# Holding input loads and a weight load behind two transposing transfers, and rearranging one quad on GpSimd

## The chip, the cores and the metric
The kernel runs on one core of a Trainium2 chip. The metric is the device time of one execution in microseconds (us). The core has TensorE (PE, matmuls; PEld is its weight load), VectorE (DVE), ScalarE (ACT), GpSimd (POOL) and SyncE (SP), and 16 DMA engines that all queues share. Three runs of the kernel before took 386.72, 385.92 and 386.15 us, so the median is 386.15 us.

## The reference
An attention with squared relu, then a two-layer block whose middle is a leaky relu with a slope for each channel:

```python
# q, k, v: 8 batches x 12 heads x 448 positions x 64
scores = scale * (q @ k^T)
attn = maximum(scores, 0) ** 2 / 448
x = (attn @ v), heads side by side           # 3584 tokens x 768
h = x @ w_in                                 # 768 -> 2048
g = maximum(h, 0) + alpha * minimum(h, 0)
out = g @ w_out                              # 2048 -> 768, float32
```

## The kernel before
The unit of attention is a **quad**: four heads of one batch, so three quads for each batch and 24 in all. `load_qk(n)` and `load_v(n)` (lines 94 and 103) bring a quad's q, k and v from HBM; GpSimd issues these DMAs, and they turn float32 into bf16 on the way. Each tensor of a quad is 224 KB in bf16. The buffers `raw` for q and k are three deep each, `v` seven deep.

The scores need q and k with the 64 channels on the partitions. The first five quads are transposed on TensorE (`turn_pe`, line 149). From quad 5 on it is `turn_dma` (line 161): VectorE copies q and k into a buffer `perm` in another order of rows (line 164, two copies), then SyncE issues one transposing DMA from `perm` to a tile `T` (line 166). `perm` has two buffers, `T` four. The text calls the tile of quad 5 T[5], and so on.

`sc` computes score chunks: four matmuls (line 178) and a relu on ScalarE or VectorE (lines 187 and 189). `sq` squares them (line 197 on VectorE, line 195 on ScalarE). `attnv(n)` multiplies by v (line 207) and evicts half of the result on ScalarE (line 217) and half on VectorE (line 218) into `xT`. `f1(b, ff)` is the first layer for 128 of 2048 channels (matmuls at line 241, `f1_out` at lines 249 and 250). `f2(sb, c, h)` is the second layer for 128 tokens and one of two column groups of the output, h = 0 being the first 256 columns and h = 1 the other 512 (matmuls at line 266, 16 for each group, then a ScalarE copy at line 268 and two output DMAs from SyncE at line 274). The weights of h = 1 are the tile `w_out1`, loaded by `load_w_out(1)` (line 120) in four DMAs of 512 KB, of which each serves four of the 16 matmuls of a group in turn.

The order of the work is written out by hand; each engine takes its instructions in program order, and one that waits holds up all behind it. GpSimd's stream holds nearly only DMA issues. Line 376 is the exception: a copy of one element of T[5] into the tile `landed`. It has no other use than that GpSimd waits there until the transposing transfer of quad 5 is complete, and that what stands behind it on GpSimd is issued later. Before this copy stand the loads of q and k of quad 6 and q of quad 7 (lines 374 and 375); behind it k of quad 7, quad 8, `load_w_out(1)`, and v of quad 6.

Around the change, TensorE does this (lines 368 to 446): f1 of batch 0 to its end, f2(0,0,0), scores of quad 4, attnv(3), f2(0,1,0), f2(0,2,0), scores of quad 5 (the first use of T[5], line 396), attnv(4), the beginning of f1 of batch 1 (lines 418 to 421; it reads xT of quads 3 and 4), the rest of quad 5, attnv(5), f1 of batch 1, f2(0,3,0), scores of quad 6 (line 440, the first use of T[6]), f2(0,0,1) (line 441, the first use of w_out1). The transposing transfers of quads 7 and 8 are called from inside f1 of batch 1 (line 436).

The lines of the section that the change touches:

```python
    load_qk(6)
    load_qk(7, "q")
    nc.gpsimd.tensor_copy(landed, T[5][:1, 0, 0, :1])
    load_qk(7, "k")
    load_qk(8)
    load_w_out(1)
    load_v(6)
```

Of the kernel before, what the change touches and what calls it, by code (L numbers as in the profile page):

```python
# [20 lines left out]
def kernel(  # L21
# [10 lines left out]
    nc = tc.nc  # L32
# [12 lines left out]
    singles = ctx.enter_context(tc.tile_pool(name="singles", bufs=1))  # L45
    raw_pool = ctx.enter_context(tc.tile_pool(name="raw", bufs=3))
    v_pool = ctx.enter_context(tc.tile_pool(name="v", bufs=7))
    perm_pool = ctx.enter_context(tc.tile_pool(name="perm", bufs=2))
    T_pool = ctx.enter_context(tc.tile_pool(name="T", bufs=4))
    rl_pool = ctx.enter_context(tc.tile_pool(name="rl", bufs=7))  # L50
    at_pool = ctx.enter_context(tc.tile_pool(name="at", bufs=12))
# [11 lines left out]
    landed = singles.tile([1, 1], BF16)  # L63
# [22 lines left out]
    def take_bank():  # L86
        i = min(range(8), key=lambda i: (taken[i], i))
        take(i, 1)
        return psum[:, i]


    raw, vraw = {}, {}

    def load_qk(n, names="qk"):
        b, g = divmod(n, NG)
        for name in names:
            src = q if name == "q" else k
            t = raw_pool.tile([128, 2, NJ, D], BF16, tag=name, name=f"{name}raw")
            flat = src[b].rearrange("(m two) (pp j) d -> (two pp) m (j d)", two=2, j=NJ)
            nc.gpsimd.dma_start(out=t.rearrange("p m j d -> p m (j d)"), in_=flat[:, 2 * g:2 * g + 2])  # L100
            raw[(n, name)] = t

    def load_v(n):
        b, g = divmod(n, NG)
        t = v_pool.tile([128, 2, NJ, D], BF16, tag="v", name="vraw")
        flat = v[b].rearrange("(m two) (pp j) d -> (two pp) m (j d)", two=2, j=NJ)
        nc.gpsimd.dma_start(out=t.rearrange("p m j d -> p m (j d)"), in_=flat[:, 2 * g:2 * g + 2])  # L107
        vraw[n] = t
# [11 lines left out]
    def load_w_out(h, lo=0, hi=KF, step=4):  # L120
        for lo in range(lo, hi, step):
            nc.gpsimd.dma_start(out=w_out_sb[h][:, lo:lo + step], in_=w_out_v[:, lo:lo + step, COLS[h][0]:COLS[h][1]])
# [24 lines left out]
    T = {}  # L147
# [10 lines left out]
            copy = nc.vector.tensor_copy if eng == "D" else nc.scalar.copy  # L158
            copy(dst, ps[:, 128 * lo:128 * hi])  # L159

    def turn_dma(n):
        p = perm_pool.tile([128, 2, NJ, 2, D], BF16, tag="perm", name="perm")
        for i, name in enumerate("qk"):
            nc.vector.tensor_copy(p[:, i], raw.pop((n, name)).rearrange("p s j d -> p j s d"))  # L164
        t = T_pool.tile([128, 2, NJ, 128], BF16, tag="T", name="T")
        nc.sync.dma_start_transpose(out=t.rearrange("p a j c -> p (a j) c"),
                                    in_=p.rearrange("p a j s d -> p (a j s d)"))
        T[n] = t
# [53 lines left out]
    def sc(chunks):  # L222

        for n, j, eng in chunks:
            late.append((n, j, relu(score_mm(n, j), eng)))

    def sq(k=99, eng="D"):
        for g in late[:k]:
            square(*g, eng)
        del late[:k]  # L230
# [28 lines left out]
    def f2(sb, c, h, parts=None):  # L259

        first_col, width = COLS[h][0], COLS[h][1] - COLS[h][0]
        o = o_pool.tile([128, d_model - CUT], F32, tag="o", name="osb")
        for lo, hi in parts or ((0, width),):
            ps = take_bank()[:, :hi - lo]
            for ff in range(KF):
                nc.tensor.matmul(ps, gT[sb][:, ff, bass.ts(c, 128)], w_out_sb[h][:, ff, lo:hi],  # L266
                                 start=(ff == 0), stop=(ff == KF - 1))
            nc.scalar.copy(o[:, lo:hi], ps)  # L268
            for u in range(2):
                blk = 2 * c + u  # L270
                b, j = 2 * sb + blk // NJ, blk % NJ
                rows = out[b * S:(b + 1) * S].rearrange("(pp j) d -> j pp d", j=NJ)
                eng = nc.scalar if u and parts else nc.sync
                eng.dma_start(out=rows[j][:, first_col + lo:first_col + hi], in_=o[64 * u:64 * u + 64, lo:hi])  # L274
# [4 lines left out]
    def ch(n, lo, hi, p=pat):  # L279
        return [(n, j, p[j]) for j in range(lo, hi)]  # L280
# [61 lines left out]
    def f1s(b, lo, hi):  # L342
        for ff in range(lo, hi):
            f1(b, ff)
# [6 lines left out]
    def prepare(n):  # L351
        if n < NQ:
            turn_dma(n)
        load(n + 2)
# [11 lines left out]
    f1s(0, 10, 12)  # L366
    sc(ch(3, 6, 7) + ch(4, 0, 2, "AA"))
    turn_dma(5)
    f1s(0, 12, 13)
    kept = late[:]  # L370
    del late[:]
    f1s(0, 13, 16)
    late += kept
    load_qk(6)
    load_qk(7, "q")
    nc.gpsimd.tensor_copy(landed, T[5][:1, 0, 0, :1])
    load_qk(7, "k")
    load_qk(8)
    load_w_out(1)
    load_v(6)  # L380
    f2(0, 0, 0)
    sq()
    sc(ch(4, 2, 5, "AAADAAA"))
# [2 lines left out]
    sq(3)  # L386
    sq(2, "A")
    sq()
    turn_dma(6)
    load_qk(9)  # L390
    load_v(7)
    load_v(8)
    load_v(9)
    f2(0, 1, 0)
    f2(0, 2, 0)
    sc(ch(5, 0, 3))
    sq(1)
    attnv(4)
# [117 lines left out]
```

## Time and profile before
| | |
|---|---|
| median of three runs | 386.15 us (385.92 to 386.72) |
| the profiled execution | 386.72 us |
| its span | 384.8 us, so 1.92 us lie around it |
| DVE, ACT, POOL busy | 266.0, 206.8 and 67.9 us |
| granted TensorE clock | 0.999 |
| T[5]: issued by SyncE, landed | at 43.33 us, 10.6 us later |
| T[6]: issued by SyncE, landed | at 53.71 us, 6.4 us later |
| last quarter of w_out1: landed | 17.1 us after its issue at about 58.9 us |

Times in the trace are counted from the span's start. A line of a timeline gives start, duration, engine, source line and operation, what is written from what, the number of instructions merged into it, and in brackets the idle time before it with what ended it. The list of waits gives the total, the number and the longest. The DMA view for a stretch of time gives, for each queue, its packets, megabytes and the share of the 16 engines' time: q0 carries the DMAs that GpSimd issues ("software"), q1 those of SyncE and ScalarE ("hardware"). Megabytes are those of the bf16 written.

### The profile page before, as it was taken

The numbers are of one execution on the slowest core, as the hardware profiler recorded it, in microseconds if no ns is written. First come the engines' busy times: TensorE is split into PE (matmuls) and PEld (weight loads), VectorE is DVE, ScalarE is ACT, GpSimd is POOL, SyncE is SP. The second block draws the span as 40 slices with busy tenths as digits, with TensorE's granted clock in tenths as the row PEclk, the third lists the DMA queues.
The fourth block names the chain that finished last, engine by engine and source line by source line (L and its number), as shares of the span: only waits on it lengthen the run. The fifth ranks groups of instructions, "written<-read, shape, count | busy, mean of one in ns | idle before, by whom it ended". The sixth has DMA issues, their size and how long they took to land.

```text
span 384.8 us, 7838 instructions
## 1 busy us (share of the span) xinstructions
PE 374.6 (97%) x3178; PEld 205.4 (53%) x3200; DVE 266.0 (69%) x422; ACT 206.8 (54%) x331; POOL 67.9 (18%) x102
## 2 busy tenths in 40 slices
PE   7799999999999999999999999999999999999996
PEld 6444554545554455545465455544556445645554
DVE  4987987765777988689655897779855788526300
ACT  5978686446364664565444655537544375434321
POOL 8557235132202202022200222020000000000000
PEclk9999999999999999999999999999999999999999
DMA  9999999999993666698292872946035300120023
GB/s 160 189 202 201 201 129 207 176 193 227 179 191 49 113 123 102 110 141 119 45 162 61 140 122 46 171 67 127 17 82 91 77 0 16 43 68 2 14 68 84
DMA packets 73284, 43.42 MB, mean 113 GB/s; under 512 B 40352, under 2 KB 69792, under 8 KB 73248
## 3 DMA queue, kind: packets, MB, share of 16 engines
q0 software_dynamic: 26864, 22.45, 39.6%
q1 hardware_dynamic: 45952, 20.07, 27.0%
q8 instruction: 25, 0.41, 0.4%
q10 hardware_dynamic: 432, 0.39, 0.3%
q14 instruction: 11, 0.09, 0.1%
HBM read 45.62 MB, written 11.01 MB: 147 GB/s over the span
## 4 chain that ended last, share of the span: by engine, by line
PE 89%; DMA 6%; DVE 3%; issue 1%; ACT 0%; ACTq 0%
PE psum L266 37%; PE psum L241 36%; PE psum L178 8%; PE psum L207 8%; DMA T<-perm 3%; DMA kraw<-in_k_dram 2%; DVE at L197 2%; DMA qfirst<-in_q_dram 1%; PE psum L156 1%; DVE T L159 1%; DVE rl L189 1%; ACT osb L268 0%; ACTq L274 0%; DVE qraw L140 0%; ACT T L159 0%
## 5 line engine op out<-in xcount | busy, mean ns | idle before, releaser
L266 PE MATMUL psum<-w_out,gT 128*128 128x256 bf16 (+3 forms) x890 | 149.8, 322 | 1.2
L241 PE MATMUL psum<-xT,w_in_sb 128*128 128x448 bf16 x768 | 150.0, 353 | 0.0
L266 PEld LDWEIGHTS <-gT 128*128 128x128 bf16 x912 | 86.7, 98 | 64.2 <-issue 8.2
L241 PEld LDWEIGHTS <-w_in_sb 128*128 128x128 bf16 x768 | 73.5, 98 | 73.0 <-issue 5.7
L250 DVE SCALAR_TENSOR_TENSOR gT<-neg,beta_sb,psum 128x448 bf16<-128x448 f32 x128 | 83.5, 677 | 35.8 <-ACT neg L249 35.8
L249 ACT ACTIVATE neg<-psum 128x448 f32<-128x448 f32 x128 | 69.2, 546 | 61.5 <-PE psum L241 60.3
L187 ACT ACTIVATE rl<-psum 128x896 bf16<-128x896 f32 x113 | 97.9, 931 | 2.2 <-PE psum L178 2.2
L197 DVE TENSOR_TENSOR at<-rl 128x896 bf16<-128x896 bf16 x164 | 91.6, 617 | 0.0
L189 DVE TENSOR_SCALAR rl<-psum 128x896 bf16<-128x896 f32 x55 | 59.7, 1086 | 40.0 <-PE psum L178 39.9
L268 ACT COPY osb<-psum 128x256 f32<-128x256 f32 (+3 forms) x57 | 26.9, 473 | 104.5 <-PE psum L266 98.7
L178 PE MATMUL psum<-T 64*64 64x448 bf16 x672 | 44.7, 356 | 3.6 <-DVE T L159 1.1
L100 POOL DMA_DIRECT2D qraw<-in_q_dram x23 | 16.6, 721 | 157.1 <-DVE perm L164 148.4
L207 PE MATMUL psum<-at,vraw 64*64 64x448 bf16 x672 | 36.6, 350 | 0.3 <-DVE at L197 0.2
L178 PEld LDWEIGHTS <-T 64*64 64x64 bf16 x672 | 16.6, 106 | 22.2 <-issue 12.5
L207 PEld LDWEIGHTS <-vraw 64*64 64x64 bf16 x672 | 20.9, 106 | 12.6 <-issue 2.3
L218 DVE TENSOR_SCALAR xT<-psum 128x448 bf16<-128x448 f32 x23 | 14.3, 624 | 14.5 <-PE psum L207 10.9
L107 POOL DMA_DIRECT2D vraw<-in_v_dram x24 | 17.5, 729 | 7.1 <-DMA w_out<-in_moe_w_out_dram 4.1
L100 POOL DMA_DIRECT2D kraw<-in_k_dram x23 | 16.6, 722 | 6.2 <-DMA w_out<-in_moe_w_out_dram 3.2
L217 ACT ACTIVATE xT<-psum 128x448 bf16<-128x448 f32 x23 | 12.6, 549 | 2.7 <-PE psum L207 2.7
L164 DVE COPY perm<-qraw 128x896 bf16<-128x896 bf16 x19 | 11.6, 611 | 0.0
L164 DVE COPY perm<-kraw 128x896 bf16<-128x896 bf16 x19 | 11.5, 608 | 0.0
L117 POOL DMA_DIRECT2D w_in_sb<-in_moe_w_in_dram x16 | 10.1, 633 | 7.4 <-DMA w_in_sb<-in_moe_w_in_dram 2.8
(25 smaller groups left out, 40.4 us busy)
## 6 DMA issues: line engine op xcount, KB each, us to landing
out_dram<-osb SPq DMA_DIRECT2D x54, 128.0 KB, 2.4
vraw<-in_v_dram POOLq DMA_DIRECT2D x24, 224.0 KB, 8.2
qraw<-in_q_dram POOLq DMA_DIRECT2D x23, 224.0 KB, 5.4
kraw<-in_k_dram POOLq DMA_DIRECT2D x23, 224.0 KB, 6.8
out_dram<-osb SPq DMA_DIRECT2D x56, 64.0 KB, 2.2
w_in_sb<-in_moe_w_in_dram POOLq DMA_DIRECT2D x16, 192.0 KB, 8.9
w_out<-in_moe_w_out_dram POOLq DMA_DIRECT2D x4, 512.0 KB, 12.4
w_out<-in_moe_w_out_dram POOLq DMA_DIRECT2D x4, 256.0 KB, 8.9
```

The source lines that it names most:

```text
L100: nc.gpsimd.dma_start(out=t.rearrange("p m j d -> p m (j d)"), in_=flat[:, 2 * g:2 * g + 2])
L164: nc.vector.tensor_copy(p[:, i], raw.pop((n, name)).rearrange("p s j d -> p j s d"))
L178: nc.tensor.matmul(ps[64 * c:64 * c + 64, r, :S], t[64 * r:64 * r + 64, 1, j, 64 * c:64 * c + 64], t[64 * r:64 * r + 64, 0, :, 64 * c:64 * ...
L187: nc.scalar.activation(rl, ps[:, :, :S], ACTF.Relu)
L189: nc.vector.tensor_scalar(rl, ps[:, :, :S], 0.0, None, ALU.max)
L197: nc.vector.tensor_tensor(a, rl, rl, ALU.mult)
L207: nc.tensor.matmul(ps[64 * s:64 * s + 64, r, :S], vv[64 * r:64 * r + 64, s, j, :], a[64 * r:64 * r + 64, s], start=(j == 0), stop=(j == NJ ...
L241: nc.tensor.matmul(ps, w_in_sb[:, km // 2, km % 2, bass.ts(ff, 128)], xT[b][:, km // 2, km % 2, :], start=(km == 0), stop=(km == KM - 1))
L249: nc.scalar.activation(neg, ps, ACTF.Relu, scale=-1.0)
L250: nc.vector.scalar_tensor_tensor(gT[b // 2][:, ff, (b % 2) * S:(b % 2) * S + S], neg, beta_sb[:, ff:ff + 1], ps, ALU.mult, ALU.add)
L266: nc.tensor.matmul(ps, gT[sb][:, ff, bass.ts(c, 128)], w_out_sb[h][:, ff, lo:hi], start=(ff == 0), stop=(ff == KF - 1))
L268: nc.scalar.copy(o[:, lo:hi], ps)
```

## The change
One buffer more for `perm`. The copy that waits for T[5] moves ahead of all loads of quads 6 to 8. The two copies that rearrange quad 6 are made by GpSimd, right behind these loads, and v of quads 6 and 7 is loaded behind them. The transposing transfer of quad 6 is issued behind f2(0,1,0) and f2(0,2,0), which puts it behind four output DMAs on SyncE. A second copy of one element into `landed` makes GpSimd wait for T[6]; w_out1 is loaded behind it, then quad 9 and v of quads 8 and 9. The streams of TensorE and ScalarE keep their order.

```diff
-    perm_pool = ctx.enter_context(tc.tile_pool(name="perm", bufs=2))
+    perm_pool = ctx.enter_context(tc.tile_pool(name="perm", bufs=3))
...
-    def turn_dma(n):
+    def rearrange_rows(n, eng):
         p = perm_pool.tile([128, 2, NJ, 2, D], BF16, tag="perm", name="perm")
         for i, name in enumerate("qk"):
-            nc.vector.tensor_copy(p[:, i], raw.pop((n, name)).rearrange("p s j d -> p j s d"))
+            eng.tensor_copy(p[:, i], raw.pop((n, name)).rearrange("p s j d -> p j s d"))
+        return p
+
+    def turn_dma(n, p=None):
+        p = p or rearrange_rows(n, nc.vector)
         t = T_pool.tile([128, 2, NJ, 128], BF16, tag="T", name="T")
...
     late += kept
+    nc.gpsimd.tensor_copy(landed, T[5][:1, 0, 0, :1])
     load_qk(6)
-    load_qk(7, "q")
-    nc.gpsimd.tensor_copy(landed, T[5][:1, 0, 0, :1])
-    load_qk(7, "k")
+    load_qk(7)
     load_qk(8)
-    load_w_out(1)
+    rows6 = rearrange_rows(6, nc.gpsimd)
     load_v(6)
+    load_v(7)
     f2(0, 0, 0)
...
     sq()
-    turn_dma(6)
+    f2(0, 1, 0)
+    f2(0, 2, 0)
+    turn_dma(6, rows6)
+    nc.gpsimd.tensor_copy(landed, T[6][:1, 0, 0, :1])
+    load_w_out(1)
     load_qk(9)
-    load_v(7)
     load_v(8)
     load_v(9)
-    f2(0, 1, 0)
-    f2(0, 2, 0)
     sc(ch(5, 0, 3))
```

## The prediction, made blind
> **What bounds the kernel now.** First the page: the span and the engines.
>
> ```profile
> span 384.8 us, 7838 instructions
> ## 1 busy us (share of the span) xinstructions
> PE 374.6 (97%) x3178; PEld 205.4 (53%) x3200; DVE 266.0 (69%) x422; ACT 206.8 (54%) x331; POOL 67.9 (18%) x102
> ```
>
> TensorE is busy for 374.6 of 384.8 us, so everything that a change of loads and engines can win lies in the 10.2 us in which it is not. Most of those are at the ends: the first matmuls on data start at 5.45 us, and behind the last there is only output. Next I read the list of TensorE's waits for DMAs, and the timeline of TensorE where the change sits.
>
> ```profile
> PE psum L178 <- DMA T<-perm: 0.7, 1, 0.7
> ```
> ```profile
> 49.59 3.67 PE L266 MATMUL psum<-w_out,gT 128*128 128x256 bf16 x32
> 53.93 0.76 PE L178 MATMUL psum<-T 64*64 64x448 bf16 x12 [0.67 <-DMA T<-perm]
> ...
> 76.66 1.91 PE L266 MATMUL psum<-w_out,gT 128*128 128x256 bf16 x16
> 78.50 0.76 PE L178 MATMUL psum<-T 64*64 64x448 bf16 x12
> 79.19 2.98 PE L266 MATMUL psum<-w_out,gT 128*128 128x512 bf16 x12
> ```
>
> There is one wait for a transfer: scores of quad 5 are ready to start at 53.26 and start at 53.93, when T[5] lands. From there TensorE runs without a gap that matters; at 78.50 it uses T[6] and at 79.26 w_out1, both long landed (60.1 and 76.0 us). So **0.67 us is all that can be seen to win**, and two deadlines follow it. GpSimd's timeline shows the order that the change alters:
>
> ```profile
> 42.65 0.71 POOL L100 DMA_DIRECT2D qraw<-in_q_dram  x1 [0.46 <-issue]
> 53.94 0.18 POOL L376 COPY landed<-T 1x1 bf16<-1x1 bf16 x1 [10.58 <-DMA T<-perm]
> 54.42 0.71 POOL L100 DMA_DIRECT2D kraw<-in_k_dram  x1 [0.30 <-PE psum L178]
> 55.29 0.71 POOL L100 DMA_DIRECT2D qraw<-in_q_dram  x1
> 56.00 0.72 POOL L100 DMA_DIRECT2D kraw<-in_k_dram  x1
> 56.71 3.00 POOL L122 DMA_DIRECT2D w_out<-in_moe_w_out_dram  x4
> ```
>
> **T[5] earlier.** Before, q6, k6 and q7 are issued at 40.33, 41.48 and 42.65, just ahead of T[5] at 43.33. The DMA view shows no hardware packet at all from 43.3 to 47.0, while the software queue moves 0.73 MB; from 46.2 to 53.9 it moves another 0.68 MB beside T[5]. Three loads of 224 KB are 0.69 MB: without them the software queue is empty at about 46.2. A transposing transfer left nearly alone takes 2.6 us (stretch 125.0 to 127.6: 1794 hardware packets). So T[5] lands between 46.2 + 2.6 = 48.8 and 53.9 (if its late start is not the queue's doing); I take 47.0 + 2.6 = 49.6, the nearer row. TensorE needs it at 53.26: **0.67 us goes**, and no part of these 3.7 us of margin is worth more, because TensorE is busy with f2(0,2,0) until 53.26.
>
> **Loads of quads 6 to 8.** The first issue follows the landing by 0.48 us (53.94 to 54.42), each issue takes 0.72: q6 at 50.1, the last (k8) issued by 54.4. A load on quiet queues lands 4.1 to 4.3 us after its issue (those at 131.99 and 121.94). Behind it one more lands each 224 KB / 0.203 MB per us = 1.1 us (stretch 62.6 to 69.4, below). So q6 lands at 54.3, k6 at 55.4, k8 at about 60. Quads 7 and 8 are needed by VectorE at 64.6 and 72.4: hidden.
>
> **Rearranging on GpSimd.** The trace has no such copy there. On VectorE it took 0.61 us. Of GpSimd's own rows, the copy of one element took 177 ns and the 128-element select 287 ns, so (287 - 177) / 127 = 0.87 ns an element and 0.177 + 895 x 0.00087 = 0.96 us for 896; the select alone scaled by 7 gives 2.0 us. Bounds 0.61 to 2.0; I take 0.96, which has the fixed part taken out. Two copies behind k8's issue, the second behind k6's landing: done at about 56.5 (58.5 at 2.0 each). VectorE loses two copies, 1.14 us from 52.50 to 53.64, but then stood idle 0.99 us for scores of quad 5: worth nothing. The third `perm` buffer costs nothing; it only takes away a wait.
>
> **T[6] later.** It is issued at 56.5 instead of 53.71, behind four outputs on SyncE that are ready by 53.7, so they do not hold it. Beside it run q7 to k8 and v6 and v7 (GpSimd issues these from 56.5; all loads drain by 60 + 2 x 1.1 = 62.2) and four outputs of 64 KB, 1.3 us. Lower end: 6.4 us to landing as now, 62.9. Upper end: all the rest first, 62.2 + 1.3 + 2.6 = 66.1. I take 64.5, between them because packets of two busy queues alternate (76 to 80 us: 700 software, 703 hardware). Needed at 78.50 - 0.67 = 77.8: hidden by 13 us.
>
> **w_out1 behind T[6].** This is the added wait that counts. Queued behind it on GpSimd are four issues of w_out1, then quad 9, v8, v9, and from `load(10)` on everything. Two stretches of before show its rate, first alone, then beside T[7]:
>
> ```profile
> q0 software_dynamic: 1403, 1.38, 122.5%
> q1 hardware_dynamic: 47, 0.03, 2.0%
> ```
> ```profile
> q0 software_dynamic: 819, 0.81, 92.0%
> q1 hardware_dynamic: 712, 0.18, 38.2%
> ```
>
> These are 62.6 to 69.4 and 69.4 to 75.6 us: columns are packets, MB and share. Alone 1.38 MB / 6.8 us = 0.203 MB per us, beside T[7] 0.131. Before, w_out1 (2.1 MB) moved in these 13.0 us. After, T[7], issued at about 65, runs beside it whole and T[8] in part: 2.1 / 0.203 = 10.3 plus one transposing transfer of 2.6 is 12.9; all at the slower rate it is 16.0. With T[6] at 64.5: first issue at 65.0, first bytes 1.1 later (the load issued at 131.99 moves nothing until 133.0), 13.0 of moving (the measured row, near the lower end), 0.4 to the landing: 79.5. The last quarter is needed by matmul 13 of f2(0,0,1), 78.6 + 12 x 0.23 = **81.3**. Hidden, with 1.8 us to spare; at the ends of the range the landing is 77.8 or 84.1. Quad 9 then lands at about 82.5; VectorE wants it at 85.3, and T[9] is used only at 107. v8 is needed at 113.
>
> **The sum** against the profiled execution: 386.72 - 0.67 = 386.05, say 386.1 us. That execution was the slowest of the three, 0.57 above the median of 386.15, so some of its wait may be absent in the others; the forecast stands at -0.02% of the median. About 0.2% (0.77 us) is what a measurement of this kernel can tell from no change: faster means under 385.38, slower over 386.92.
>
> **Rival 1, w_out1 becomes the wait (slower).** Place: matmul 13 of f2(0,0,1). For it: a GpSimd stream shut for some 7 us, and DMA engines busy through all of 60 to 95 us. Against it: 1.8 us of margin. It begins when T[6] lands after 66.3 and makes the kernel slower when that is after 67.2 (0.87 us late), or at 64.5 when moving takes over 15.7 instead of 13.0. With T[6] at the upper end of 66.1 and 14.5 of moving the last quarter lands at 82.6, 1.3 late: 387.4. At both upper ends it lands at 84.1, 2.8 late: 388.9.
>
> **Rival 2, GpSimd holds up VectorE (slower).** VectorE's rows there, and the matmuls that wait for them:
>
> ```profile
> 55.63 0.62 DVE L197 TENSOR_TENSOR at<-rl 128x896 bf16<-128x896 bf16 x1
> 56.17 0.62 DVE L218 TENSOR_SCALAR xT<-psum 128x448 bf16<-128x448 f32 x1
> ```
> ```profile
> 56.33 1.69 PE L241 MATMUL psum<-xT,w_in_sb 128*128 128x448 bf16 x8
> ```
>
> The fourth of these matmuls (at 56.33 + 0.6 = 56.93) reads the xT that is written by 56.79: a margin of 0.14 us. All moves 0.67 earlier, so the square at 55.63 comes at 54.96, in the middle of GpSimd's copies (54.4 to 56.5). What the two do to each other no row shows; bounds: nothing, and one whole copy, 0.96 - 0.14 = 0.8 or 2.0 - 0.14 = 1.9 us. I take nothing to 0.3, since the first copy should end near 55.4. It turns the kernel slower from 1.0 us of hold-up: 387.3 in the middle of 386.9 to 388.0.
>
> The Trainium skill speaks for this rival: SBUF — State Buffer, "Who interferes with whom", says that VectorE and GpSimd share one pair of ports as an exclusive lock held for a whole instruction, and names VectorE operations with two SBUF inputs against GpSimd ones that read SBUF. The square is one. By that rule a copy of 0.96 us that starts just ahead of it costs 0.8 us, a total of 386.9; without the rule 386.1. No run here shows it yet.
>
> **Rival 3, T[5] does not come earlier.** If its 4 us to the first packet is its own and not the queue's, TensorE still waits: 386.2 to 386.7. Against it: T[6], issued into emptier queues, took 6.4 us.
>
> **Rival 4, a gain beyond 0.2%.** If each run holds the 0.67 us and the spread lies at the start and the end, 385.92 to 386.72 becomes 385.25 to 386.05; with VectorE's lost 1.14 us worth a little, 385.2.
>
> **How the numbers follow.** Forecast 0.34 and rival 3 0.08 are within 0.2%: 0.42. Rival 1 0.23 and rival 2 0.15 are slower: 0.38. Rival 4 is faster: 0.20. The range must reach both sides: 385.2 cuts rival 4 in half (0.1 out), 387.9 cuts the worse part of rivals 1 and 2 (0.1 out). The likeliest case alone is 385.7 to 386.9.
>
> **What would show it.** T[5] landing near 50 and no wait of line 182 (178 now) for it; GpSimd's two copies near 1 us each; T[6] landing between 62.9 and 66.1; the wait of f2(0,0,1) for a DMA, none in my forecast; the margin of xT at the fourth matmul. I am wrong if f2(0,0,1) waits over 0.9 us, or if the copies take over 2 us or stop VectorE.

## The result, and the profile after

Twelve executions of the changed kernel took 388.64 us in the median (387.00 to 391.43), fifteen of the kernel before beside them 386.21. The ratio is **1.0064, interval 1.0043 to 1.0085: slower**, and outside the range of 385.2 to 387.9. The profiled execution took 387.19, span 385.3: it is one of the shortest of the twelve, so its losses are small ones. A second profiled execution, below, took 390.26 and shows large ones. Ratios here and below are not quotients of the medians, and they leave out slow executions, of which there is one, 394.42 us in run e1 below, whose median counts it.

The page and TensorE's list of waits for transfers:

```profile
span 385.3 us, 7839 instructions
...
PE 375.2 (97%) x3178; PEld 205.9 (53%) x3200; DVE 265.3 (69%) x420; ACT 206.7 (54%) x331; POOL 70.0 (18%) x105
```
```profile
PE psum L270 <- DMA w_out<-in_moe_w_out_dram: 0.8, 1, 0.8
```

The wait for T[5] is gone and one for w_out1 has come; the source lines are four further down now (178 is 182, 266 is 270). The timeline of TensorE shows where:

```profile
53.32 0.76 PE L182 MATMUL psum<-T 64*64 64x448 bf16 x12
...
55.71 1.91 PE L245 MATMUL psum<-xT,w_in_sb 128*128 128x448 bf16 x8
...
78.81 2.76 PE L270 MATMUL psum<-w_out,gT 128*128 128x512 bf16 x11
82.32 1.02 PE L270 MATMUL psum<-w_out,gT 128*128 128x512 bf16 x4 [0.75 <-DMA w_out<-in_moe_w_out_dram]
83.28 0.76 PE L182 MATMUL psum<-T 64*64 64x448 bf16 x12
```

The last four matmuls of f2(0,0,1) wait 0.75 us for the last quarter of w_out1. The books of this one execution: the scores of quad 5 start 0.61 us earlier (53.32 against 53.93); the eight matmuls at 55.71 take 1.91 instead of 1.69, so that 0.38 is left at f2(0,0,1) (78.81 against 79.19); the wait costs 0.75. That makes it 0.37 longer behind f2(0,0,1), and the whole execution is 0.47 longer.

GpSimd's timeline, in which the new order can be followed, then the chain of waits between 50 and 90 us:

```profile
49.71 0.18 POOL L378 COPY landed<-T 1x1 bf16<-1x1 bf16 x1 [10.81 <-DMA T<-perm]
50.20 0.71 POOL L100 DMA_DIRECT2D qraw<-in_q_dram  x1 [0.31 <-issue]
...
54.46 0.99 POOL L164 COPY perm<-qraw 128x896 bf16<-128x896 bf16 x1
55.68 1.04 POOL L164 COPY perm<-kraw 128x896 bf16<-128x896 bf16 x1 [0.23 <-DMA kraw<-in_k_dram]
56.68 1.43 POOL L107 DMA_DIRECT2D vraw<-in_v_dram  x2
67.45 0.18 POOL L396 COPY landed<-T 1x1 bf16<-1x1 bf16 x1 [9.34 <-DMA T<-perm]
67.89 2.98 POOL L122 DMA_DIRECT2D w_out<-in_moe_w_out_dram  x4 [0.27 <-issue]
```
```profile
56.75 10.57 DMA T<-perm
...
70.11 12.17 DMA w_out<-in_moe_w_out_dram
```

Read from the end: the last quarter of w_out1 is issued at 70.11 and lands at 82.28; GpSimd could not issue it earlier, because T[6], issued at 56.75, lands only at 67.32.

### The profile page after: what moved, and what is told of

It reads as the page before. It is cut to its first block, busy times and chain, and to the rows that moved or that the text cites. A ratio compares the mean times of both kernels' runs of the same rounds, so it can differ in the third digit from the quotient of the medians.

```text
span 385.3 us, 7839 instructions
## 1 busy us (share of the span) xinstructions
PE 375.2 (97%) x3178; PEld 205.9 (53%) x3200; DVE 265.3 (69%) x420; ACT 206.7 (54%) x331; POOL 70.0 (18%) x105
## 4 chain that ended last, share of the span: by engine, by line
PE 80%; DMA 10%; issue 4%; DVE 3%; POOL 1%; ACT 0%; ACTq 0%; POOLq 0%
PE psum L270 35%; PE psum L245 30%; PE psum L182 7%; PE psum L211 7%; DMA w_out<-in_moe_w_out_dram 5%; DMA T<-perm 3%; DVE at L201 2%; DMA kraw<-in_k_dram 1%; DMA qfirst<-in_q_dram 1%; DVE T L159 1%; DVE rl L193 1%; PE psum L156 1%; POOL w_out L122 0%; POOL perm L164 0%; POOL qraw L100 0%
## 5 line engine op out<-in xcount | busy, mean ns | idle before, releaser
L254 DVE SCALAR_TENSOR_TENSOR gT<-neg,beta_sb,psum 128x448 bf16<-128x448 f32 x128 | 83.5, 677 | 35.6 <-ACT neg L253 35.5
L253 ACT ACTIVATE neg<-psum 128x448 f32<-128x448 f32 x128 | 69.2, 546 | 61.2 <-PE psum L245 59.4
```

What stands on the lines that cost most here:

```text
L253: nc.scalar.activation(neg, ps, ACTF.Relu, scale=-1.0)
L254: nc.vector.scalar_tensor_tensor(gT[b // 2][:, ff, (b % 2) * S:(b % 2) * S + S], neg, beta_sb[:, ff:ff + 1], ps, ALU.mult, ALU.add)
```

## The experiments

Times in the table are from each run's profiled execution, in us from the start of its span; "issued" for w_out1 is the first of its four DMAs, "landed" the last. TensorE wants that last quarter at 80.8 to 81.7 in most runs, at about 82 in the kernel before, f5 and g2 and at 84.7 in e2, where it was held up earlier, and at 84.1 in e4. Ratios are to the kernel before, run on the same chip.

| kernel | T[6] issued, landed | w_out1 issued, landed | wait for w_out1 | median | ratio (interval) |
|---|---|---|---|---|---|
| before | 53.7, 60.1 | 56.7, 76.0 | none | 386.2 | 1 |
| changed | 56.7, 67.3 | 67.9, 82.3 | 0.75 | 388.64 | 1.0064 (1.0043 to 1.0085) |
| changed, second profile | 57.1, 68.5 | 69.1, 83.8 | 2.28 | | |
| e1: w_out1 behind v7, no wait | 57.5, 74.5 | 58.8, 84.0 | 2.40 | 390.81 | 1.0089 (1.0060 to 1.0118) |
| e4: use of w_out1 later | 57.6, 68.8 | 69.3, 84.2 | 0.15 | 386.79 | 1.0012 (1.0001 to 1.0024) |
| e2: hold alone | 57.7, 74.4 | 54.8, 75.1 | none | 388.62 | 1.0056 (1.0036 to 1.0075) |
| f5: wait for T[6] alone | 54.2, 60.8 | 61.3, 78.1 | none | 386.24 | 1.0001 (0.9993 to 1.0010) |
| f6: GpSimd's rows alone | 57.9, 74.7 | 57.9, 76.5 | none | 387.39 | 1.0030 (1.0020 to 1.0040) |
| g3: rows and wait, no hold | 57.7, 64.3 | 64.9, 82.1 | 0.89 | 387.57 | 1.0046 (1.0024 to 1.0068) |
| f4: v6, v7 behind w_out1 | 57.1, 64.0 | 64.6, 81.9 | 0.93 | 387.49 | 1.0035 (1.0023 to 1.0047) |
| f1: w_out1 first, no wait | 57.1, 74.5 | 57.0, 76.4 | none | 386.46 | 1.0008 (0.9999 to 1.0017) |
| g2: f1, rows on VectorE, late | 57.8, 75.4 | 54.5, 76.4 | none | 386.57 | 1.0007 (0.9999 to 1.0016) |
| g1: one load moved | 53.5, 67.8 | 55.2, 83.1 | 2.19 | 388.97 | 1.0059 (1.0028 to 1.0090) |
| h1: changed, copies before q7 | 56.7, 63.2 | 63.7, 83.5 | 0.32 + 2.12 | 387.92 | 1.0050 (1.0032 to 1.0069) |
| h2: g1 with the order restored | 53.4, 59.4 | 57.0, 76.8 | none | 385.83 | 0.9993 (0.9984 to 1.0002) |

My first theory was rival 1 in its plainest form: the wait for T[6] makes w_out1 late. Against it stood rival 2 (GpSimd holds up VectorE) and, later, that the hold (GpSimd's loads of quads 6 to 8 held back until T[5] has landed) does the harm.

**e1: the wait for T[6] removed.**

```diff
     load_v(7)
+    load_w_out(1)
...
     turn_dma(6, rows6)
-    nc.gpsimd.tensor_copy(landed, T[6][:1, 0, 0, :1])
-    load_w_out(1)
```

> As the changed kernel, but w_out1 is issued right behind v7 and waits for nothing; quad 9, v8 and v9 follow it. Theory (the last quarter of w_out1 lands too late because its issue waits for T[6]): the wait of f2(0,0,1) for a DMA is gone, the time is 385.7 to 386.4 us and its spread falls below 1 us. T[6] then shares the DMA engines with w_out1 and lands later, up to 74 us, which nobody notices before 77.8. Rival (GpSimd's copies holding up VectorE are the loss): the time stays above 387.5 us with its spread.

A miss. Issued 9.1 us earlier than in the changed kernel, w_out1 lands 1.7 us later, at 84.0. Early issue is no early landing: T[6] and w_out1 now move side by side, both are late (T[6] by 7.2 us), and the kernel is slower still. The theory in that form fell.

**A second profile of the changed kernel.**

> The changed kernel once more, for its profile. Theory: the only wait of TensorE for a DMA behind 50 us is that of f2(0,0,1) for the last quarter of w_out1, and it differs from 0.75 us by as much as the span differs from 385.3 us; T[6] lands at 67 us or later. Rival: the span varies with something else, and this wait stays at 0.7 to 0.8 us.

It took 390.26 us, 3.07 more than the first. TensorE's timeline:

```profile
83.80 1.02 PE L270 MATMUL psum<-w_out,gT 128*128 128x512 bf16 x4 [2.28 <-DMA w_out<-in_moe_w_out_dram]
84.75 1.12 PE L182 MATMUL psum<-T 64*64 64x448 bf16 x12
85.81 8.36 PE L270 MATMUL psum<-w_out,gT 128*128 128x512 bf16 x32
```

T[6] lands at 68.5, w_out1 at 83.8: a wait of 2.28 instead of 0.75, 1.53 more. The rest is in the other two lines: 12 scores at 1.12 instead of 0.76 and 32 matmuls at 8.36 instead of 7.08, 1.64 more, with the granted clock at 0.50 from 85 to 88 us. The expectation had the whole difference in the wait; it is about half of it, and the cost of a late w_out1 counts twice in an execution like this.

**e4: the use moved.** Two groups of f2 change places, so that w_out1 is wanted later. The expectation speaks of f2(0,4,0) and f2(0,5,0) ahead, 4.5 us; the kernel that ran moves f2(0,4,0) alone, some 2.5 us.

```diff
     run(some(3))
-    f2(0, 0, 1)
+    f2(0, 4, 0)
...
     run(some(3))
-    f2(0, 4, 0)
+    f2(0, 0, 1)
```

> As the changed kernel, but the second layer takes its groups in another order: f2(0,4,0) and f2(0,5,0) come ahead of f2(0,0,1), so that w_out1 is first used about 4.5 us later. All loads stay where the change put them. Theory (w_out1 misses a deadline): most of the loss is gone, 385.8 to 386.8 us. Rival (the loss is on VectorE and GpSimd, or in the DMA engines as such): 387.5 us or more, as for the changed kernel.

w_out1 lands as late as ever, 84.2, but it is wanted only at 84.1: TensorE stops for 0.15 us, and 388.64 becomes 386.79. So some three quarters of the loss (1.85 of 2.43 us) are the missed deadline of w_out1.

**e2, f5, f6, g3: the parts alone.**

e2, the loads of quads 6 to 8 behind the landing of T[5]:

```diff
-    load_qk(6)
-    load_qk(7, "q")
     nc.gpsimd.tensor_copy(landed, T[5][:1, 0, 0, :1])
-    load_qk(7, "k")
+    load_qk(6)
+    load_qk(7)
     load_qk(8)
```

f5, w_out1 behind the landing of T[6]:

```diff
     load_qk(8)
-    load_w_out(1)
...
     turn_dma(6)
+    nc.gpsimd.tensor_copy(landed, T[6][:1, 0, 0, :1])
+    load_w_out(1)
```

f6, GpSimd rearranging quad 6, with the third buffer; g3 has the edits of f5 and f6:

```diff
     load_w_out(1)
+    rows6 = rearrange_rows(6, nc.gpsimd)
     load_v(6)
...
-    turn_dma(6)
+    turn_dma(6, rows6)
```

> The kernel before with one part of the change alone: all loads of quads 6 to 8 behind the wait for T[5]; VectorE rearranges quad 6, w_out1 waits for nothing. Theory: T[5] lands near 50 and TensorE's wait for it, 0.67 us, is gone, but VectorE reaches the copies of quad 6 at about 52.5 and must wait for k6 until about 55.5, with the relus and squares of quad 5 queued behind; TensorE loses about 2 us there and none at w_out1: 387.3 to 388.7 us. Rival (the early wait is free whoever rearranges): 385.6 to 386.2 us.

> The kernel before with one part of the change alone: w_out1 is issued behind a wait for T[6]; q6, k6 and q7 are loaded ahead of T[5] as before, VectorE rearranges quad 6. Theory V: T[6] lands at about 60 as before, w_out1 is issued at 60.6 and its last quarter lands by 77.5 to 79.5 us, before 82.0 when it is wanted: same time as before, 385.9 to 386.5 us. Theory W: the added wait costs 1 us or more by itself, 387 us or more.

> The kernel before with one part of the change alone: GpSimd rearranges quad 6 (behind k8's issue, ahead of w_out1), with the third buffer. The two copies take 0.9 to 1.05 us each and run from about 56.7 to 58.7 us, where VectorE squares quad 5: a square beside a copy takes 0.9 to 1.05 instead of 0.62 us, two of them 0.3 to 0.8 us in all, of which TensorE feels up to 0.5 us at attnv(5). Both theories: w_out1 is issued 2 us later, lands by 78 us, no wait; the wait for T[5] stays; 386.0 to 386.9 us. A time above 387.2 us would say that GpSimd's copies are a loss of their own.

> The changed kernel without the hold: quad 6 and q7 are loaded ahead of the landing of T[5] as in the kernel before, GpSimd rearranges quad 6, w_out1 waits for T[6]. Theory (the loss of the changed kernel needs hold and wait together, for only the hold puts the loads of quad 6 to 8 between the two transfers): T[6] lands near 62 to 64, w_out1's last quarter at 79 to 80.5, no wait for it; what stays is the lock on VectorE and the wait for T[5] that before has, 386.3 to 386.9. Rival (GpSimd's rearranging alone costs the 1.2 us that the run with it alone had, through its hold-up of VectorE): 387.2 to 387.6 again, though T[6] is early here.

The hold alone does what was expected: T[5] lands at 50.0, and VectorE, whose copies now wait for k6 until 57.0, stops TensorE:

```profile
58.70 0.38 PE L178 MATMUL psum<-T 64*64 64x448 bf16 x4 [3.12 <-DVE rl L189]
```

The wait for T[6] alone is free, as expected: T[6] lands at 60.8 because VectorE's copies let SyncE issue it at 54.2. GpSimd's rows alone cost 1.2 us (387.39), more than the 386.9 at the upper end. A second profile of that kernel (386.98 us against 385.98 beside it) shows one part of why:

> A second look at the kernel before with GpSimd rearranging quad 6 as its only change, whose median was 387.39 although its profiled execution took 386.66. If the rest is TensorE waiting for T[6] (landed 74.7 in the first look, used at 78.1), this execution shows T[6] landing after 78 and a wait of line 182 for it of up to 1 us. If it is w_out1 (landed 76.5, needed at 81.3), a wait of line 270 for it. If it is GpSimd holding up VectorE, no wait for a DMA, and the square of quad 4 or the matmuls behind it later by 0.5 us or more than in the first look.

```profile
98.74 0.76 PE L182 MATMUL psum<-T 64*64 64x448 bf16 x12 [0.27 <-DMA T<-perm]
```

None of the three places that I had named: it is T[8], which lands at 98.7 (92.9 before) and is used at 98.5. T[6] is issued 4.1 us later and lands at 74.9, and T[7] and T[8], behind it in the same queue, land later too. This wait is 0.27; that it is longer in the slower executions was not seen.

g3 was the test of "hold and wait together", and that theory fell: without the hold, T[6] lands at 64.3, just behind the 62 to 64 that was expected, yet w_out1 lands at 82.1 (expected 79 to 80.5) and TensorE waits 0.89. The 387.57 is the rival's number, but not its reason, since the rival had no such wait. T[7], issued at 65.2, lands at 80.8: it runs beside w_out1 from first to last. In the changed kernel T[7] had landed at 69.4, straight behind T[6] and just as the first packets of w_out1 came, and w_out1 then had the engines to itself until 77. Counted as in the prediction, from 1.1 us behind the first issue to 0.4 ahead of the landing, w_out1 moved for 12.9 us there (69.0 to 81.9) and for 15.7 here (66.0 to 81.7). (The first packets really come 1.5 us behind the issue in both, so each figure holds 0.4 us too much.)

**f4, f1, g2: other places for w_out1.**

All three start from the changed kernel. f4:

```diff
     rows6 = rearrange_rows(6, nc.gpsimd)
-    load_v(6)
-    load_v(7)
...
     load_w_out(1)
+    load_v(6)
+    load_v(7)
```

f1:

```diff
     rows6 = rearrange_rows(6, nc.gpsimd)
+    load_w_out(1)
     load_v(6)
...
     turn_dma(6, rows6)
-    nc.gpsimd.tensor_copy(landed, T[6][:1, 0, 0, :1])
-    load_w_out(1)
```

g2, against f1:

```diff
-    rows6 = rearrange_rows(6, nc.gpsimd)
     load_w_out(1)
...
-    turn_dma(6, rows6)
...
     attnv(4)
+    turn_dma(6)
```

> As the changed kernel, wait for T[6] and all, but v6 and v7 are loaded behind w_out1. Theory V: T[6] shares the DMA engines with two loads less, lands at 64 to 65.5 instead of 67.3 to 68.5, and w_out1 lands by 79 to 81 us; TensorE waits 0 to 0.5 us; 385.7 to 386.5 us, though w_out1 still waits for T[6]. Theory W: the wait for T[6] keeps its price and the kernel stays above 387 us.

> As the changed kernel, but w_out1 is issued right behind GpSimd's two copies, ahead of v6 and v7, and waits for nothing. Theory V (what decides is how much data stands ahead of the last quarter of w_out1 once T[5] has landed; the change puts five loads of 224 KB more there than before): v6 and v7, 0.45 MB, now come behind w_out1; at the 0.15 MB per us that the software queue moves beside a transposing transfer that is 3 us, so the last quarter lands at about 81 instead of 84.0 us (the kernel without the wait for T[6]); TensorE waits 0 to 0.6 us; 385.9 to 386.8 us. Theory W (the wait for T[6] was the loss) is already weakened: without the wait the kernel was slower still. Theory W would give 385.7 to 386.4 for this one as well; a wait above 1.5 us here would speak against both.

> The changed kernel with w_out1 issued behind k8 with no wait for T[6], ahead of v6 and v7, and quad 6 rearranged by VectorE behind quad 4's attention (copies near 57 to 58.5) instead of by GpSimd. Theory (what is left of the loss in the run with w_out1 first, 0.3 us, is GpSimd holding up VectorE's square): square back at 0.62 us, 385.7 to 386.2, if T[6], issued 1.5 us later, still lands before 77.9. Rival (it is not the lock but T[6] landing near the time of its use): T[6] lands at 75 to 78, 386.4 or more, with a wait of line 182 for it in some executions.

f4: T[6] lands at 64.0 as expected, and again w_out1 needs until 81.9 with T[7] beside it: a wait of 0.93 and 387.49, where 385.7 to 386.5 was expected. f1 removes the wait and puts w_out1 ahead of v6 and v7: it lands at 76.4, where about 81 was expected, and the loss is gone but for 0.25 us, which the interval can't tell from nothing. T[6] moves beside w_out1 there, lands only at 74.5, and nothing waits for it. f1 and e1 differ only in two loads of 224 KB ahead of w_out1, and in 7.6 us of its landing; at the 0.15 MB per us of the expectation the two loads are 3 us, and the rest is not explained. g2 was to show whether VectorE's hold-up is those 0.25 us. It can't tell: its VectorE copies make TensorE wait 1.26 us for a relu at 58.78, and its median is the same.

**g1: one load moved, nothing else.**

```diff
     load_qk(6)
-    load_qk(7, "q")
     nc.gpsimd.tensor_copy(landed, T[5][:1, 0, 0, :1])
-    load_qk(7, "k")
+    load_qk(7)
```

> The kernel before with one load alone moved: q7 is issued behind the landing of T[5] instead of ahead of it (q6 and k6 stay ahead, VectorE rearranges quad 6, w_out1 is free). Theory (the change pays too dearly for 0.67 us, since five loads of 224 KB are put behind the landing where one is enough): T[5] lands 1.1 us earlier, near 52.8, no wait of line 178 for it, w_out1's last quarter lands 0.7 later, near 76.7, no wait for it; 385.6 to 386.2. Rival (the 0.67 us of the profiled execution of before are its own, other executions have none): no difference, 386.1 to 386.4.

A miss, and the most telling run. T[5] lands at 51.8 and its wait is gone, but T[6], issued at 53.5 as before, lands at 67.8 instead of 60.1, and w_out1 at 83.1 instead of 76.0:

```profile
83.16 1.44 PE L266 MATMUL psum<-w_out,gT 128*128 128x512 bf16 x4 [2.19 <-DMA w_out<-in_moe_w_out_dram]
```

With an early T[5], GpSimd's next loads are issued from 52.4, ahead of T[6]; before, they were issued from 54.42, behind it. So moving one load moved the whole of GpSimd's stream behind it some 2 us forward. Three of its nine executions took 386.0 to 386.4 all the same, the others 387.6 to 391.7: the loss does not come each time, and why is not known, as only a long one was profiled.

**h2 and h1: the order of T[6] and the loads.** h2 is g1 with one more copy of one element, on the rows that VectorE writes for T[6], ahead of q7. h1 is the changed kernel with GpSimd's copies ahead of q7.

h2:

```diff
-    nc.gpsimd.tensor_copy(landed, T[5][:1, 0, 0, :1])
-    load_qk(7)
-    load_qk(8)
-    load_w_out(1)
-    load_v(6)
...
-    turn_dma(6)
+    rows6 = rearrange_rows(6, nc.vector)
+    turn_dma(6, rows6)
+    nc.gpsimd.tensor_copy(landed, T[5][:1, 0, 0, :1])
+    nc.gpsimd.tensor_copy(landed, rows6[:1, 1, 0, 0, :1])
+    load_qk(7)
+    load_qk(8)
+    load_w_out(1)
+    load_v(6)
```

h1:

```diff
     load_qk(6)
+    rows6 = rearrange_rows(6, nc.gpsimd)
     load_qk(7)
     load_qk(8)
-    rows6 = rearrange_rows(6, nc.gpsimd)
```

> The run with one load moved (q7 behind the landing of T[5], 388.97), with one more wait ahead of q7: a one-element copy on GpSimd that reads the rows of quad 6 which VectorE rearranges for T[6], so that q7, k7, q8, k8 and w_out1 are issued at about 54.0, behind T[6]'s issue at 53.5, instead of from 52.4. Theory (what the kernel before got from its late T[5] is that T[6] is issued ahead of the next loads and has the DMA engines to itself): T[6] lands near 60 to 61 instead of 67.8, w_out1's last quarter near 76.5 instead of 83.1, no wait for T[5] and none for w_out1; 385.8 to 386.3. Rival (the landing of T[6] does not depend on a lead of 1.5 us): T[6] and w_out1 as in the run with one load moved, 388 to 389.5.

> The changed kernel with GpSimd's two copies of quad 6 put right behind the loads q6 and k6, so that q7, k7, q8, k8, v6 and v7 are issued behind them, at about the time of T[6]'s own issue (56.7). Theory (T[6] landed at 67.3 instead of 64.5 because loads that were already moving shared the DMA engines with it; loads issued no earlier than T[6] leave it alone for some 4 us, as in the kernel before): T[6] lands at 61 to 63, w_out1 is issued from 61.5 to 63.5 behind the six loads, its last quarter lands at 79.5 to 81.5, no wait for it or one under 0.3 us; 386.2 to 386.9, the hold-up of VectorE staying. Rival (a transposing transfer issued this late takes 10 us whatever moves beside it): T[6] again at 67, w_out1 at 82 to 84, 387.5 to 389.

h2 is as its theory said, and the rival (that a lead of 1.5 us can't matter) falls. GpSimd's timeline shows the added wait, and that its loads stand behind T[6]'s issue at 53.4:

```profile
52.14 0.22 POOL L389 COPY landed<-T 1x1 bf16<-1x1 bf16 x1 [10.71 <-DMA T<-perm]
53.50 0.18 POOL L390 COPY landed<-perm 1x1 bf16<-1x1 bf16 x1 [1.14 <-DVE perm L164]
54.02 0.72 POOL L100 DMA_DIRECT2D qraw<-in_q_dram  x1 [0.34 <-PE psum L182]
```

Holding q7 and all behind it on GpSimd back by 1.6 us (q7 from 52.39 to 54.02) makes T[6] land 8.4 us earlier (59.4) and w_out1 6.4 earlier (76.8); neither T[5] nor w_out1 is waited for, and 388.97 becomes 385.83, the fastest median of all, though within 0.2% of the kernel before. The DMA view for 60 to 64 us, first g1, then h2 (packets, MB, share):

```profile
DMA packets 849, 0.36 MB, mean 90 GB/s; under 512 B 630, under 2 KB 849, under 8 KB 849
...
q1 hardware_dynamic: 622, 0.16, 90.0%
q0 software_dynamic: 227, 0.20, 64.1%
```
```profile
DMA packets 1054, 0.89 MB, mean 223 GB/s; under 512 B 111, under 2 KB 1054, under 8 KB 1054
...
q0 software_dynamic: 766, 0.66, 101.7%
q1 hardware_dynamic: 288, 0.23, 22.5%
```

The DMA engines are busy through these 4 us in both. Where T[6] and loads meet, they move 0.36 MB; where T[6] is over, 0.89 MB. What is not moved there lands later.

h1 confirms the first half: with the other loads issued from T[6]'s own issue on, it lands 6.4 us after that (56.7 to 63.2), as in the kernel before, where the changed kernel took 10.6. The four outputs ahead of T[6] land earlier too, so h1 does not tell the loads from the outputs. Its second half was a miss: w_out1, though issued at 63.7, lands at 83.5. Six loads of 224 KB stand ahead of it in the queue until 69.0, and T[7] (64.8 to 82.4) runs beside it.

## Why the prediction was wrong

The theory that the runs leave standing: behind the wait for T[6], w_out1 starts too late for its deadline once transposing transfers and bulk loads meet in the DMA engines. **The step that failed is the landing of T[6]**: "I take 64.5", at most 66.1. Measured 67.3, 68.5 and 68.8 in three executions of the changed order. What stands behind it in the sum came out in number: GpSimd's copy 0.13 after the landing, 0.44 to the first issue, about 13 us of moving. Put 67.3 in the place of 64.5 and the working gives 79.5 + 2.8 = 82.3, which is what the trace has. Rival 1 even named the point, slower "when that is after 67.2".

But the 13.0 us of moving agreed by luck. The prediction had T[7] beside w_out1 "whole" and still took 13.0, a stretch of the kernel before in which T[7] ran beside w_out1 only for the last 6.2 us (69.4 to 75.6); in the changed kernel T[7] was over when w_out1 began. Where T[6] did land as forecast, at 64.0 (f4) and 64.3 (g3), T[7] ran beside w_out1, which moved for 15.7 us, and TensorE waited 0.93 and 0.89. Rival 1 had this condition too ("at 64.5 when moving takes over 15.7 instead of 13.0"). TensorE in f4:

```profile
81.90 1.02 PE L270 MATMUL psum<-w_out,gT 128*128 128x512 bf16 x4 [0.93 <-DMA w_out<-in_moe_w_out_dram]
```

The DMA view from 73 to 77 us, first the changed kernel, then f4:

```profile
q0 software_dynamic: 814, 0.82, 123.6%
```
```profile
q0 software_dynamic: 518, 0.51, 75.7%
q1 hardware_dynamic: 512, 0.13, 27.0%
```

Where the changed kernel moves 0.82 MB of loads, f4 moves 0.51 beside T[7]. So the moving beside T[7] was too short by 2.7 us in the prediction, and a T[6] on time would not have saved the forecast: the two terms hang together, and w_out1 lands at about 82 whether T[6] lands at 64 or at 67.

Two sentences made T[6] too early. One has T[6] "behind four outputs on SyncE that are ready by 53.7, so they do not hold it": ready is not moved. The four were issued from 52.9 on, and between 52 and 57 us the changed kernel's queues look like this:

```profile
q0 software_dynamic: 860, 0.73, 108.4%
q14 instruction: 1, 0.01, 0.4%
```

Not one hardware packet, while the loads move 0.73 MB. The outputs land at 58.8 to 61.8, and the first packets of T[6] in the trace come behind 60.5, some 4 us after its issue (about 1 us in the kernel before, where no output was ahead of it). In h1, with only q6 and k6 under way, the same outputs land at 56.0 to 57.4. The other sentence is "all loads drain by 60 + 2 x 1.1 = 62.2": v7 lands at 66.2. It had one load each 1.1 us from the rate of w_out1 alone; beside outputs and T[6] they came each 1.5 to 2.6. From 61 to 65 us T[6] shares the engines with the last of them: 1059 hardware and 564 software packets.

What I had not seen in the profile of before: the late T[5] was worth something. It kept GpSimd's next loads behind T[6]'s issue, so T[6] had the DMA engines to itself (from 54 to 58 us 1592 hardware packets and no software packet) and was out of the way of w_out1. I priced T[5]'s wait at 0.67 us to be won and asked only what falls due next on TensorE, not which transfer the wait had kept apart from which. g1 and h2 show this without the rest of the change: the early T[5] is harmless when the order of T[6] and the loads is kept. It is not the meeting alone that costs: in f1 and f6 T[6] moves beside w_out1 to 74.5 and 74.7, and w_out1, issued by 58 us, lands in time (76.4 and 76.5).

Step by step:
- **T[5]** landing at 49.6, wait gone: right (49.7). But not each execution holds 0.67 us. The other profiles with the same three loads ahead of T[5] show a wait for it of 0.60 (f5), 0.20 and 0.18 (f6, twice) and none (g3), and the spans of other executions of before are mostly 383.8 to 384.6, against 384.8 for the profiled one, so there was less to win.
- **Loads**: q6 at 54.1 (54.3) and k6 at 55.6 (55.4) right; k8 at 63.1 instead of 60.
- **Rearranging**: 0.99 and 1.04 us against the 0.96 that I took, done at 56.7 against 56.5: right.
- **Rival 2** is real and small. VectorE's square takes longer in the changed kernel:

```profile
55.02 0.91 DVE L201 TENSOR_TENSOR at<-rl 128x896 bf16<-128x896 bf16 x1
```

It was 0.62. The xT behind it comes too late for the fourth matmul, and the eight take 1.91 instead of 1.69: 0.22 us, inside the "nothing to 0.3". In the second profile, where the copy is nearly over when the square begins (it ends at 55.16, the square begins at 55.06), the square takes 0.62 again; in e1 it takes 1.04.

The Trainium skill, SBUF — State Buffer, "Who interferes with whom", speaks of a lock for the whole instruction: the direction agrees (0.62 becomes 0.91 to 1.04 beside copies of 0.93 to 1.04), and the price in this trace is 0.2 us, a quarter of the 0.8 that the rule gave for the worst timing.

- **Rivals 3 and 4** did not come.
- **The size**: at both upper ends I had 388.9 for rival 1, and the median is 388.64. That agreement is luck: the 388.9 is a wait of 2.8 us from 16.0 us of moving, while the two profiles show waits of 0.75 and 2.28, and the second 1.64 more at half clock. Two things were not in it: w_out1 lands at 82.3 to 83.8 from one execution to the next, and a long wait can also cost clock.

What stays open: why T[6] and the loads move so slowly together in g1 and not in f1 or f6 (in g1 237 software and 250 hardware packets from 62 to 65 us, 478 and 481 from 77 to 80, when T[7] and w_out1 share the engines), and the part of f6's 1.2 us that is neither the hold-up nor the 0.27 us at T[8].

## What to carry to other kernels

Before you remove a wait, ask what it keeps in order: a transfer that lands late may be what lets the next critical transfer start ahead of the bulk loads, and here bringing GpSimd's loads in front of it, by moving one of 224 KB, cost 2.8 us in the median (388.97 against 386.2; three of nine executions lost nothing), while holding them back by 1.6 us won it all back, and the profile has no wait for either transfer. Price a transfer that must land by a deadline with everything already moving or queued when it is issued, not with its duration in the old order; a margin of 1.8 us is none where the landing that it rests on comes 2.8 to 4.3 us later than taken (67.3 to 68.8 against 64.5). And where two terms of a sum depend on each other, as the landing of T[6] and the traffic beside w_out1 do, work them out together. A late issue is not the same as a late landing, nor an early one an early: look at which queue has packets in each stretch.

## What the runs showed of the hardware

**Clock.** A wait of TensorE of 2.1 to 2.4 us can cost a stretch of half clock afterwards. The windows of e1 (us; busy time and count of PE, PEld, DVE, ACT, POOL; then the granted clock, DMA share, GB/s):

```profile
81.00:84.00 3.00, 0.65 (x4) 0.19 (x2) 0.26 (x1) 0.00 (x0) 0.71 (x1) 1.00 1.24 194
84.00:85.00 1.00, 0.95 (x3) 0.40 (x3) 0.00 (x0) 0.00 (x0) 0.00 (x0) 0.58 1.27 192
85.00:87.00 2.00, 2.00 (x14) 0.37 (x12) 0.21 (x1) 1.12 (x2) 1.21 (x2) 0.50 1.24 194
87.00:88.00 1.00, 1.00 (x8) 0.44 (x5) 1.00 (x2) 1.00 (x2) 0.65 (x2) 0.72 1.25 194
88.00:90.00 2.00, 2.00 (x11) 0.92 (x10) 2.00 (x5) 0.14 (x1) 0.29 (x1) 1.00 1.24 192
```

At 0.5 for what 0.58 leaves of the first microsecond (0.84), two whole ones and 0.56 of the fourth: 3.4 us. The second profile of the changed kernel (85.0 to 88.4), g1 (83.6 to 87.0) and h1 (83.2 to 86.6) give the same 3.4, each about 1.7 us lost. Yet e2's wait of 3.12 us was followed by 1.00 throughout. What differs is where the wait falls. In all four profiles the half clock begins 78.51 us behind the first full clock, which is 23 times the 3.413 us that it lasts. Counted in such steps, TensorE is busy for 1.01 us (e1, 80.75 to 84.16), 1.22, 1.23 and 1.37 us (h1) of the step just ahead; e2's wait is split between two steps, which keep 1.52 and 2.19 us. The ends of the kernels aside, no other step of the sixteen profiles is under 1.5 us. Only three of the changed kernel's twelve executions, those of 390.2 and more, have a mean clock of 0.996 or less.

The Trainium skill, TensorE: Matmul & The Clock Gate, Part 1, tells of a free-running window of 4096 cycles, about 3.4 us: the length agrees with the four stretches, and a window that does not start with the wait fits that one wait costs clock and another not. Its section "HAM oscillation — how this bites in real kernels" gives "no PE-idle gaps >~3.4µs" as the abstract rule: here waits of 2.1 to 2.4 us were enough, so the measurement decides.

**Two queues.** In most stretches in which both have work, their packets alternate one to one, whatever their size (the slow stretch of g1 at 60 to 64 us, 227 to 622, is an exception): 478 software packets of 1 KB and 481 hardware packets of 256 B between 77 and 80 us in g1. A transposing transfer, some 1790 small packets, moves in 2.6 us alone, but takes 15.7 to 17.3 us from issue to landing beside w_out1 (T[6] in e1, f1 and f6, T[7] in f4 and g3), and w_out1 moves for 15.7 us beside T[7] (g3) against 12.9 without. The Trainium skill, DMA: Bandwidth & Descriptors, "Queues, rings and completion order", says that the engines go round the queues packet by packet; it agrees with these counts.
